# A linear-attention layer and a two-layer MLP on one core: the issue order from a list schedule, and the weights loaded as fp32 on the input queue

## The chip, the core and the metric

The kernel runs on one core of one Trainium2 chip. The metric is device time in microseconds of one execution; three runs of the kernel before gave a median of 226.93 us (226.46 to 227.11). Engines are named as in the profile: PE is TensorE (PEld its weight loads), DVE is VectorE, ACT is ScalarE, POOL is GpSimd, SP is SyncE, which here only issues transfers.

## What is computed

Inputs `r`, `k`, `v`, `w` of shape (4 batches, 8 heads, 768 steps, 48), `u` of (8, 48), and two weight matrices, all fp32.

```python
for t in range(S):
    cur = einsum('bhd,bhe->bhde', u[None] * k[t], v[t])
    y[t] = einsum('bhd,bhde->bhe', r[t], state + cur)
    state = w[t][:, :, :, None] * state + einsum('bhd,bhe->bhde', k[t], v[t])
x = y as 3072 tokens x 384
h = x @ moe_w_in                  # 384 x 2048
out = maximum(0.01 * h, h) @ moe_w_out   # 2048 x 384
```

## The kernel before

**Attention** is worked in chunks of 128 steps: 24 chunks (6 for each batch, in order, as the state is handed on). For a chunk ScalarE takes the log of `w` (`s_log`, L124), TensorE makes its running sums `cum` with two triangular matrices, ScalarE the exponentials, and VectorE the decayed `rd` and `kd` (`s_decay`, L129). TensorE transposes them (`trp`), VectorE copies them out (`rkT`), TensorE makes the scores `at`, VectorE masks them into `mt`, TensorE makes `y` from state and scores and the update `kv`, VectorE the sums `ysb` and `tt`, and GpSimd the new state `st` (`s_trans` to `s_mix`, L176 to L246). The `u` term goes beside it: three products on GpSimd (`t`, twice, and `vsc`), a cast of `v` (`vb`) and a sum on VectorE (`diag`) (L153 to L171). Last `ysb` is transposed (`ytr`) and ScalarE copies it into `xT` (`s_out`, L253).

**The MLP** works on blocks of tokens; ten blocks, `sizes = [384, 128, 128, 256, 384, 384, 384, 384, 384, 256]`. `m_hidden` (L269) makes `hp` from `w_in_b` and `xT`, three matmuls for each of 16 rows of tiles, and ScalarE writes the leaky ReLU to `gt`. `m_out` (L282) makes `op` for 128 tokens from 16 matmuls with `w_out_b`, ScalarE copies it (`osb`), and it is stored. `hp` and `op` share two PSUM buffers (`ps_mlp`).

**Loads.** SyncE's queue carries the four input tiles of each chunk (196.6 KB each, rows of 48 numbers) and the stores. Eight buffers for each input hold the chunks ahead. `load_w_in` (L105) and `load_w_out` (L113) read the fp32 weights on GpSimd's queue and turn them into bf16 on the way.

**Order.** Every engine works in the order of issue. That order is written by hand: each stage of each chunk has a position, the MLP's units are spread over the positions behind the chunks that they need, and all are sorted.

```python
def when(i, s):
    if i < 3:
        return 5 * i + s
    ...
    return 5 * i + 3 * s
...
events.append((when(2, 0) + 0.3, 0, 0, load_w_in, ()))
events.append((when(2, 0) + 0.4, 0, 0, load_w_out, ()))
```

The identity matrix `ident`, which the transposes need, is made on GpSimd at the program's start; its last step stands there behind the first product of chunk 0, which needs `u`.

Of the kernel before, what the change touches and what calls it, by code (L numbers as in the profile page):

```python
# [8 lines left out]
F32 = mybir.dt.float32  # L9
# [3 lines left out]
AX = mybir.AxisListType  # L13


@with_exitstack
def kernel(
# [47 lines left out]
    ident = const.tile([128, 128], BF16, name="ident")
    make_identity(nc, ident)
    ones = const.tile([128, 1], BF16, name="ones")
    nc.vector.memset(ones[:], 1.0)

# [5 lines left out]
    for t in lw_b + rd_b + kd_b:  # L75
        nc.vector.memset(t[:, :, D:64], 0.0)
    for t in st_b:
        nc.vector.memset(t[:], 0.0)

    nc.scalar.preload_act_table_set("natural_log_exp_and_others")  # L80

# [4 lines left out]


    ins = {}

    def load_chunk(i):  # L90
        b, c = divmod(i, C)
        t0 = c * L
        tiles = {}
        for name, src in (("w", w), ("r", r), ("k", k), ("v", v)):
            t = inpool.tile([128, H, D], F32, name=f"{name}_in", tag=f"{name}_in")
            nc.sync.dma_start(
                out=t[:], in_=src[b, :, t0 : t0 + L, :].rearrange("h p d -> p h d")
            )
            tiles[name] = t
        ins[i] = tiles  # L100
# [4 lines left out]
    def load_w_in():  # L105
        fq = FF // 4
        for q in range(4):
            nc.gpsimd.dma_start(
                out=w_in_b[:, :, q * fq : (q + 1) * fq],
                in_=moe_w_in[:, q * fq : (q + 1) * fq].rearrange("(t p) n -> p t n", p=128),  # L110
            )

    def load_w_out():  # L113
        hf = NFT // 2
        for q in range(2):
            nc.gpsimd.dma_start(
                out=w_out_b[:, q * hf : (q + 1) * hf, :],
                in_=moe_w_out[q * hf * 128 : (q + 1) * hf * 128, :].rearrange("(t p) n -> p t n", p=128),
            )


    att = {}

    def s_log(i):  # L124
        a = att[i] = ins.pop(i)
        a["lw"] = lw_b[i % NB3]
        nc.scalar.activation(out=a["lw"][:, :, 0:D], in_=a["w"][:], func=AF.Ln)  # L127

    def s_decay(i):  # L129
        c = i % C  # L130
        a = att[i]
        lw, rd, kd = a["lw"], rd_b[i % NB3], kd_b[i % NB3]
        a["rd"], a["kd"] = rd, kd
        cum = ps_cum.tile([128, 1024], F32, name="cum")
        nc.tensor.matmul(cum[:, 128:512], lhsT=tri[:], rhs=lw[:, :, 0:D], start=True, stop=True)  # L135
        nc.tensor.matmul(cum[:, 512:896], lhsT=trin[:], rhs=lw[:, :, 0:D], start=True, stop=True)  # L136
        for p in range(NP):
            nc.tensor.matmul(  # L138
                cum[:, 896 + p : 897 + p],
                lhsT=lw[:, 2 * p : 2 * p + 2, :].rearrange("p h d -> p (h d)"),  # L140
                rhs=ones[:], start=True, stop=True,
            )
        nc.scalar.activation(out=cum[:, 128:900], in_=cum[:, 128:900], func=AF.Exp)  # L143
        e1 = cum[:, 128:512].rearrange("p (h d) -> p h d", h=H)
        e2 = cum[:, 512:896].rearrange("p (h d) -> p h d", h=H)
        nc.vector.tensor_tensor(out=rd[:, :, 0:D], in0=e1, in1=a["r"][:], op=ALU.mult)  # L146
        nc.vector.tensor_tensor(out=kd[:, :, 0:D], in0=e2, in1=a["k"][:], op=ALU.mult)  # L147
        if c < C - 1:
            el = work.tile([128, NP], F32, name="el")
            nc.vector.tensor_copy(out=el[:], in_=cum[:, 896:900])  # L150
            a["el"] = el

    def s_prod(i):  # L153
        a = att[i]
        t1 = work.tile([128, DM], F32, name="t1", bufs=2)
        nc.gpsimd.tensor_tensor(out=t1[:], in0=a["r"][:].rearrange("p h d -> p (h d)"), in1=ukb[:], op=ALU.mult)  # L156
        t2 = work.tile([128, H, D], F32, name="t2", bufs=2)
        nc.gpsimd.tensor_tensor(  # L158
            out=t2[:], in0=t1[:].rearrange("p (h d) -> p h d", h=H), in1=a["k"][:], op=ALU.mult
        )  # L160
        a["t2"] = t2
        vb = work.tile([128, DM], BF16, name="vb")
        nc.gpsimd.tensor_copy(out=vb[:], in_=a["v"][:].rearrange("p h d -> p (h d)"))
        a["vb"] = vb

    def s_diag(i):
        a = att[i]
# [209 lines left out]
```

## Time and profile before

| what | value |
|---|---|
| median of 3 runs | 226.93 us |
| profiled execution | 227.73 us |
| its span, first to last instruction | 225.7 us |
| TensorE busy | 188.8 us (84%) |
| VectorE, ScalarE, GpSimd busy | 105.8, 109.6, 104.5 us |
| read and written in HBM | 25.36 MB, 4.72 MB |

All times within a profile count from the start of the span. How the rows of the next sections read: in a table of stretches, each row has the stretch, its length, then for PE, PEld, DVE, ACT and POOL the busy time with the number of instructions, then the granted TensorE clock (1.00 is full speed), the share of the DMA engines and GB/s. In a timeline a row has start, length, engine, line, operation, output<-input, shape, count, and in brackets the idle time before it with what ended it; rows of the queue of SyncE are marked SPq, and their length is that of the issue. A row of the chain has start, length, engine, name, line and count; its first line gives shares of the stretch. In rows by line, the last numbers are busy time and mean length in ns, then idle time before.

### The profile page before, as it was taken

The numbers are of one execution on the slowest core, as the hardware profiler recorded it, in microseconds if no ns is written. First come the engines' busy times: TensorE is split into PE (matmuls) and PEld (weight loads), VectorE is DVE, ScalarE is ACT, GpSimd is POOL, SyncE is SP. The second block draws the span as 40 slices with busy tenths as digits, with TensorE's granted clock in tenths as the row PEclk, the third lists the DMA queues.
The fourth block names the chain that finished last, engine by engine and source line by source line (L and its number), as shares of the span: only waits on it lengthen the run. The fifth ranks groups of instructions, "written<-read, shape, count | busy, mean of one in ns | idle before, by whom it ended". The sixth has DMA issues, their size and how long they took to land.

```text
span 225.7 us, 4666 instructions
## 1 busy us (share of the span) xinstructions
PE 188.8 (84%) x1816; PEld 124.0 (55%) x1816; DVE 105.8 (47%) x220; ACT 109.6 (49%) x217; POOL 104.5 (46%) x152
## 2 busy tenths in 40 slices
PE   1135454996995999899999999999999999999992
PEld 1123232554583867756666666666666666556761
DVE  2344361142450797767665476645756574420000
ACT  3111202682262655645863685478538833672540
POOL 2434597005183357776835457658175557110000
PEclk9999999999999699999999999999999999999998
DMA  7999999999898999888678566300021001100101
GB/s 132 198 189 186 188 180 181 187 184 198 160 196 214 227 164 195 180 147 182 135 134 170 139 119 100 107 35 3 0 73 37 3 23 47 38 0 35 73 0 71
DMA packets 107142, 27.24 MB, mean 121 GB/s; under 512 B 100336, under 2 KB 107120, under 8 KB 107120
## 3 DMA queue, kind: packets, MB, share of 16 engines
q1 hardware_dynamic: 103440, 23.80, 56.3%
q0 software_dynamic: 3680, 3.15, 8.7%
q8 instruction: 14, 0.23, 0.5%
q14 instruction: 8, 0.07, 0.1%
HBM read 25.36 MB, written 4.72 MB: 133 GB/s over the span
## 4 chain that ended last, share of the span: by engine, by line
PE 52%; ACT 2%; issue 0%; ACTq 0%
PE op L288 21%; PE hp L276 20%; PE trp L181 2%; PE at L195 2%; ACT gt L280 1%; PE y L221 1%; PE cum L135 1%; PE ytr L257 1%; PE cum L136 1%; PE y L215 1%; PE kv L234 1%; PE cum L138 0%; ACT osb L294 0%; ACT xT L258 0%; ACTq L294 0%
## 5 line engine op out<-in xcount | busy, mean ns | idle before, releaser
L276 PE MATMUL hp<-xT,w_in_b 128*128 128x384 bf16 (+2 forms) x480 | 78.2, 302 | 4.6 <-ACT osb L294 2.8
L280 ACT ACTIVATE gt<-hp 128x384 bf16<-128x384 f32 (+1 forms) x120 | 60.6, 512 | 22.2 <-PE hp L276 20.5
L288 PE MATMUL op<-w_out_b,gt 128*128 128x384 bf16 x384 | 69.0, 326 | 1.7 <-DMA w_out_b<-in_moe_w_out_dram 1.4
L276 PEld LDWEIGHTS <-w_in_b 128*128 128x128 bf16 x480 | 41.6, 100 | 24.3 <-issue 9.1
L288 PEld LDWEIGHTS <-gt 128*128 128x128 bf16 x384 | 35.5, 98 | 22.8 <-issue 2.2
L171 POOL TENSOR_TENSOR vsc<-v_in,diag 128x384 f32<-128x384 f32 x24 | 19.9, 829 | 47.0 <-DVE diag L169 47.0
L246 POOL TENSOR_TENSOR st<-tt,el 48x192 bf16<-48x192 f32 x40 | 20.1, 502 | 37.4 <-DVE tt L241 29.5
L201 DVE TENSOR_TENSOR mt<-at,tri 128x512 bf16<-128x512 f32 x48 | 30.7, 682 | 10.9 <-PE at L195 10.9
L146 DVE TENSOR_TENSOR rd<-cum,r_in 128x384 bf16<-128x384 f32 x24 | 13.4, 556 | 43.2 <-ACT cum L143 43.1
L294 ACT COPY osb<-op 128x384 f32<-128x384 f32 x24 | 11.5, 478 | 43.3 <-PE op L288 37.3
L156 POOL TENSOR_TENSOR t<-r_in,ukb 128x384 f32<-128x384 f32 x24 | 23.9, 997 | 7.8 <-DMA ukb<-in_u_dram 6.4
L258 ACT COPY xT<-ytr 128x384 bf16<-128x384 bf16 x24 | 11.4, 476 | 31.7 <-PE ytr L257 31.6
L227 DVE TENSOR_TENSOR ysb<-y,vsc 128x384 bf16<-128x384 f32 x24 | 13.4, 557 | 25.5 <-PE y L221 15.8
L143 ACT ACTIVATE cum<-cum 128x772 f32<-128x772 f32 x24 | 19.2, 799 | 12.6 <-issue 8.3
L158 POOL TENSOR_TENSOR t<-t,k_in 128x384 f32<-128x384 f32 x24 | 23.9, 996 | 1.8
L185 DVE COPY rkT<-trp 128x1024 bf16<-128x1024 bf16 x24 | 16.5, 689 | 16.7 <-PE trp L181 16.5
L181 PE MATMUL trp<-ident,rd 128*128 128x128 bf16 x96 | 10.1, 234 | 7.5 <-POOL ident masks.py:199 4.2
L135 PE MATMUL cum<-lw,tri 128*128 128x384 bf16 x24 | 8.4, 351 | 7.9 <-ACT lw L127 7.9
L195 PE MATMUL at<-rkT 48*128 48x128 bf16 x192 | 10.6, 229 | 3.7 <-DVE rkT L185 2.4
L127 ACT ACTIVATE lw<-w_in 128x384 bf16<-128x384 f32 x24 | 12.5, 521 | 1.8 <-DMA w_in<-in_w_dram 1.8
L147 DVE TENSOR_TENSOR kd<-cum,k_in 128x384 bf16<-128x384 f32 x24 | 13.1, 548 | 0.0
L169 DVE TENSOR_REDUCE diag<-t 128x8 f32<-128x384 f32 x24 | 13.0, 543 | 0.0
(39 smaller groups left out, 147.9 us busy)
## 6 DMA issues: line engine op xcount, KB each, us to landing
w_in<-in_w_dram SPq DMA_DIRECT2D x24, 192.0 KB, 4.5
r_in<-in_r_dram SPq DMA_DIRECT2D x24, 192.0 KB, 4.5
k_in<-in_k_dram SPq DMA_DIRECT2D x24, 192.0 KB, 4.5
v_in<-in_v_dram SPq DMA_DIRECT2D x24, 192.0 KB, 4.2
out_dram<-osb SPq DMA_DIRECT2D x24, 192.0 KB, 2.0
w_in_b<-in_moe_w_in_dram POOLq DMA_DIRECT2D x4, 384.0 KB, 9.0
w_out_b<-in_moe_w_out_dram POOLq DMA_DIRECT2D x2, 768.0 KB, 18.4
ukb<-in_u_dram SPq DMA_DIRECT2D x1, 192.0 KB, 4.5
```

What stands on the lines that cost most here:

```text
L143: nc.scalar.activation(out=cum[:, 128:900], in_=cum[:, 128:900], func=AF.Exp)
L156: nc.gpsimd.tensor_tensor(out=t1[:], in0=a["r"][:].rearrange("p h d -> p (h d)"), in1=ukb[:], op=ALU.mult)
L158: nc.gpsimd.tensor_tensor(out=t2[:], in0=t1[:].rearrange("p (h d) -> p h d", h=H), in1=a["k"][:], op=ALU.mult)
L171: nc.gpsimd.tensor_tensor(out=vsc[:], in0=a["v"][:], in1=diag[:].unsqueeze(2).to_broadcast([128, H, D]), op=ALU.mult)
L181: nc.tensor.transpose(trp[:, x, p, :], src[:, 2 * p : 2 * p + 2, :].rearrange("p h d -> p (h d)"), ident[:])
L185: nc.vector.tensor_copy(out=rkT[:], in_=trp[:])
L195: nc.tensor.matmul(ats[x][:, p, :], lhsT=rkT[r0 : r0 + D, 1, p, :], rhs=rkT[r0 : r0 + D, 0, p, :], start=True, stop=True,)
L201: nc.vector.tensor_tensor(out=mt[:, x], in0=ats[x][:], in1=tri[:].unsqueeze(1).to_broadcast([128, NP, 128]), op=ALU.mult)
L246: nc.gpsimd.tensor_tensor(out=sn[r0 : r0 + D, :, x * D : (x + 1) * D], in0=tt[r0 : r0 + D, :, x * D : (x + 1) * D], in1=a["el"][r0 : r0 + ...
L276: nc.tensor.matmul(hp[:, jj, :], lhsT=w_in_b[:, t, (j + jj) * 128 : (j + jj + 1) * 128], rhs=xT[:, t, t0 : t0 + mb], start=(t == 0), stop= ...
L280: nc.scalar.activation(out=gts[q][:, j : j + nj, :], in_=hp[:], func=AF.Prelu, alpha=0.01)
L288: nc.tensor.matmul(op[:], lhsT=gts[q][:, j, ts * 128 : (ts + 1) * 128], rhs=w_out_b[:, j, :], start=(j == 0), stop=(j == NFT - 1),)
```

## The change

1. The order of issue is now made by a list schedule (`Order`). Every step is added with its engine, a planned duration, the steps it needs and the PSUM buffers it takes. `run` then picks, over all engines, the step that could start first (ties by rank: attention by chunk, then the MLP), and so writes one order. The stages are cut into single steps, such as `rd`, `kd`, `rkT`, the two masks; `op` is cut into four parts instead of two.
2. The weights are loaded as fp32 on SyncE's queue, behind the inputs of chunk 3 and ahead of those of chunk 4, in eight loads of 786 KB, into four staging buffers. ScalarE casts `w_in` (three casts a load), VectorE `w_out` (one a load). A load of `w_out` reuses a staging buffer of `w_in`.
3. There are eight blocks, `[512, 128, 256, 384, 384, 384, 512, 512]`.
4. The constants, `ident` among them, are one step at the head of GpSimd's order. The output buffers are four instead of three.

The computation is otherwise the same.

```diff
+class Order:
+    def add(self, name, eng, took, f, *args, lag=0.06, rank=0.0, needs=(), takes=()):
+        self.steps[name] = (eng, took, f, args, lag, rank, list(needs), takes)
...
+        while any(todo.values()):
+            best = None
+            for eng, names in todo.items():
...
+                for rank, seq, name in names:
...
+                    t = ready(name)
+                    if t is None:
+                        continue
+                    t = max(t, free[eng])
+                    key = (t, rank, seq)
+                    if best is None or key < best[0]:
+                        best = (key, eng, (rank, seq, name))
...
+    wpool = ctx.enter_context(tc.tile_pool(name="wpool", bufs=4))
+    opool = ctx.enter_context(tc.tile_pool(name="opool", bufs=4))
...
-    def load_w_in():
-        fq = FF // 4
-        for q in range(4):
-            nc.gpsimd.dma_start(
-                out=w_in_b[:, :, q * fq : (q + 1) * fq],
-                in_=moe_w_in[:, q * fq : (q + 1) * fq].rearrange("(t p) n -> p t n", p=128),
-            )
...
+    def load_w_in(q):
+        t = wpool.tile([128, KT, FQ], F32, name="ws", tag="ws")
+        nc.sync.dma_start(
+            out=t[:], in_=moe_w_in[:, q * FQ : (q + 1) * FQ].rearrange("(t p) n -> p t n", p=128)
+        )
+        stage["in", q] = t
...
+    def cast_w_in(q, t):
+        nc.scalar.copy(out=w_in_b[:, t, q * FQ : (q + 1) * FQ], in_=stage["in", q][:, t, :])
+
+    def cast_w_out(q):
+        nc.vector.tensor_copy(out=w_out_b[:, q * JQ : (q + 1) * JQ, :], in_=stage["out", q][:])
...
-    sizes = [384, 128, 128, 256, 384, 384, 384, 384, 384, 256]
+    sizes = [512, 128, 256, 384, 384, 384, 512, 512]
...
+    add("const", "POOL", 2.2, constants, rank=-1)
+    queue = [("in", i) for i in range(4)]
+    queue[1:1] = [("u", 0)]
+    queue += [("w_in", q) for q in range(NQ)] + [("w_out", q) for q in range(NQ)]
+    queue += [("in", i) for i in range(4, NCH)]
...
+            add((kind, n), "DMA", 2.2, f, n, lag=1.9, needs=[("cast", "w_in", n)] if kind == "w_out" else [])
...
+        step("scores", "PE", 0.35, a_scores, "rkT", lag=0.1, takes=(("att", "m0"), ("att", "m1")))
+        step("m0", "DVE", 0.66, a_mask, "scores", *past(2, "mix"), args=(0,))
...
+            add(("hid", q, j), "PE", nj * 3 * (mb / 2400 + 0.003), m_hid, q, j, nj, lag=0.1, rank=100 + q,
+                takes=(("mlp", ("act", q, j)),),
...
+                add(("out", q, ts, part), "PE", JQ * 0.163, m_out, q, ts, part, lag=0.1, rank=101.5 + q + 0.01 * ts,
...
+    steps = order.run({"att": 3, "mlp": 2})
     with tc.manual_schedule():
...
+        for f, args in steps:
+            f(*args)
```

How the order moves, at three places. First the weights' loads. Before, they stand in GpSimd's order, behind the products and the cast of chunk 2 (`t_355` is its first product):

```order
L156 TENSOR_TENSOR t_355<-r_in,ukb 128x384
L158 TENSOR_TENSOR t_357<-t_355,k_in 128x384
L163 CAST vb<-v_in 128x384
L108 DMA w_in_b<-in_moe_w_in_dram 128x3x512 x4
L116 DMA w_out_b<-in_moe_w_out_dram 128x8x384 x2
L171 TENSOR_TENSOR vsc<-v_in,diag 128x384
```

With the change they stand on SyncE's queue; `v_in_336` is the last tile of chunk 3, `w_in_541` the first of chunk 4, and `ws` are the staging buffers:

```order
L177 DMA v_in_336<-in_v_dram 128x8x48
L189 DMA ws_363<-in_moe_w_in_dram 128x3x512
L189 DMA ws_393<-in_moe_w_in_dram 128x3x512
L189 DMA ws_422<-in_moe_w_in_dram 128x3x512
L189 DMA ws_441<-in_moe_w_in_dram 128x3x512
L196 DMA ws_474<-in_moe_w_out_dram 128x4x384
L196 DMA ws_485<-in_moe_w_out_dram 128x4x384
L196 DMA ws_504<-in_moe_w_out_dram 128x4x384
L196 DMA ws_523<-in_moe_w_out_dram 128x4x384
L177 DMA w_in_541<-in_w_dram 128x8x48
```

The weights have moved from GpSimd's queue to SyncE's, between chunks 3 and 4. Second, ScalarE around the end of chunk 3 with the change (`cum_340` is the exponential of chunk 3, `ytr_397` and `ytr_467` are the outputs of chunks 2 and 3, `ws_363` to `ws_441` the four loads of `w_in`):

```order
L230 ACTIVATE cum_340<-cum_340 128x772
L203 CAST w_in_b_101<-ws_363 128x512
L350 COPY xT_103<-ytr_397 128x3x128
L203 CAST w_in_b_101<-ws_363 128x512 x2
L203 CAST w_in_b_101<-ws_393 128x512 x3
L203 CAST w_in_b_101<-ws_422 128x512 x3
L350 COPY xT_103<-ytr_467 128x3x128
L203 CAST w_in_b_101<-ws_441 128x512 x2
L376 ACTIVATE gt_479<-hp_480 128x512
```

Nine of the new casts stand ahead of the copy that completes block 0, and two more ahead of the first `gt`. Third, ScalarE's end with the change, which mirrors TensorE's there (a `gt` follows each `hp` tile, an `osb` each tile of `op`):

```order
L350 COPY xT<-ytr 128x3x128
L376 ACTIVATE gt<-hp 128x512 x5
L350 COPY xT<-ytr 128x3x128
L376 ACTIVATE gt<-hp 128x512 x11
L389 COPY osb<-op 128x384 x3
L376 ACTIVATE gt<-hp 128x512 x16
L389 COPY osb<-op 128x384 x8
```

The last 27 tiles of `hp` (blocks 6 and 7) have no attention between them now, and their `op` tiles follow in two runs.

## Rows read from the trace of the kernel before

**Rows 1.** Table of stretches, all engines.

```profile
0.00:55.00 55.00, 28.24 (x210) 16.32 (x211) 19.44 (x49) 16.33 (x30) 24.86 (x41) 1.00 1.18 182
55.00:104.27 49.27, 43.86 (x530) 32.88 (x529) 30.16 (x61) 23.52 (x44) 27.99 (x40) 0.97 1.00 188
104.27:147.89 43.62, 43.58 (x430) 28.18 (x430) 25.93 (x52) 26.82 (x56) 25.24 (x35) 1.00 0.62 126
221.54:225.70 4.16, 0.00 (x0) 0.00 (x0) 0.00 (x0) 0.48 (x1) 0.00 (x0) 0.79 0.14 49
29.20:54.00 24.80, 17.66 (x119) 9.50 (x118) 8.35 (x18) 10.33 (x21) 12.51 (x17) 1.00 1.23 185
74.00:76.00 2.00, 1.83 (x18) 1.45 (x17) 1.93 (x5) 1.56 (x4) 0.00 (x0) 0.50 1.28 210
```

**Rows 2.** Timeline of ScalarE: the logs of chunks 1 and 2.

```profile
16.28 0.53 ACT L127 ACTIVATE lw<-w_in 128x384 bf16<-128x384 f32 x1
...
26.00 0.53 ACT L127 ACTIVATE lw<-w_in 128x384 bf16<-128x384 f32 x1
```

**Rows 3.** Timeline of SyncE's queue: issues of input tiles.

```profile
15.95 0.96 SPq L96 DMA_DIRECT2D v_in<-in_v_dram  x1
16.96 1.15 SPq L96 DMA_DIRECT2D w_in<-in_w_dram  x1
...
41.77 7.05 SPq L96 DMA_DIRECT2D w_in<-in_w_dram  x1
```

**Rows 4.** The weights' tiles: issues (first and last start), and `w_out` from issue to landing.

```profile
L108 POOL DMA_DIRECT2D w_in_b<-in_moe_w_in_dram x4: 772/775/927, 29.2 to 31.6; - x4
...
L116 POOL DMA_DIRECT2D w_out_b<-in_moe_w_out_dram x2: 881/897/913, 32.4 to 33.3; - x2
...
DMA to landing us min/median/max: 16.1/18.4/20.6
```

**Rows 5.** Timeline of the head: VectorE's first product, and four places on TensorE.

```profile
6.24 0.56 DVE L146 TENSOR_TENSOR rd<-cum,r_in 128x384 bf16<-128x384 f32 x1 [4.21 <-ACT cum L143]
...
9.55 0.58 PE L181 MATMUL trp<-ident,rd 128*128 128x128 bf16 x4 [4.18 <-POOL ident masks.py:199]
...
36.78 2.08 PE L276 MATMUL hp<-xT,w_in_b 128*128 128x384 bf16 x6 [0.57 <-ACT xT L258]
...
40.59 4.03 PE L276 MATMUL hp<-xT,w_in_b 128*128 128x384 bf16 x15
...
54.01 1.46 PE L288 MATMUL op<-w_out_b,gt 128*128 128x384 bf16 x8 [1.40 <-DMA w_out_b<-in_moe_w_out_dram]
```

**Rows 6.** Timeline of TensorE: a wait ahead of 104 us, and two block starts.

```profile
94.36 0.38 PE L195 MATMUL at<-rkT 48*128 48x128 bf16 x7 [0.78 <-DVE ysb L227]
...
104.27 0.65 PE L276 MATMUL hp<-xT,w_in_b 128*128 128x384 bf16 x3 [0.33 <-ACT xT L258]
...
147.89 0.65 PE L276 MATMUL hp<-xT,w_in_b 128*128 128x384 bf16 x3
```

**Rows 7.** The chain: shares of 104.27 to 147.89, and pieces of the end.

```profile
by line: PE hp L276 38.6%; PE op L288 36.5%; PE trp L181 5.9%; PE at L195 4.5%; PE y L221 2.7%; PE ytr L257 2.3%; PE cum L135 2.2%; PE cum L136 2.2%; PE kv L234 2.0%; PE y L215 1.9%; PE cum L138 1.1%; issue 0.2%
...
199.62 0.66 PE hp L276 x3
...
207.72 2.60 PE op L288 x16
210.32 5.93 PE hp L276 x48
```

**Rows 8.** The page's DMA queue of the weights, and issue to landing of `v`.

```profile
q0 software_dynamic: 3680, 3.15, 8.7%
...
v_in<-in_v_dram SPq DMA_DIRECT2D x24, 192.0 KB, 4.2
```

**Rows 9.** Groups by line and shape: a copy on ScalarE and one on VectorE.

```profile
L280 ACT ACTIVATE gt<-hp 128x512 bf16<-128x512 f32 x24 | 14.3, 597 | 7.8 <-PE hp L276 7.2
L185 DVE COPY rkT<-trp 128x1024 bf16<-128x1024 bf16 x24 | 16.5, 689 | 16.7 <-PE trp L181 16.5
```

More of the change, by code (lines that the diff above doesn't have):

```diff
@@ L113, in load_w_out @@
[L113 to L134, printed above, removed]
+    NQ = 4
@@ L147, in s_decay @@
[L147 to L157, printed above, removed]
+            nc.tensor.matmul(cum[:, 896 + p : 897 + p], lhsT=pair(lw, p), rhs=ones[:], start=True, stop=True)
@@ L192, in s_scores, with a_rkT, a_scores @@
+    def a_rkT(i):
+        rkT = att[i]["rkT"] = work.tile([128, 2, NP, 128], BF16, name="rkT")
+        nc.vector.tensor_copy(out=rkT[:], in_=att[i]["trp"][:])
+    def a_scores(i):
+        rkT = att[i]["rkT"]
+        ats = att[i]["ats"] = [ps_att.tile([128, NP, 128], F32, name=f"at{x}", tag="att") for x in range(2)]
         for p in range(NP):
@@ new lines, in a_kv, with a_tt @@
+    def a_kv(i):
+        kv = att[i]["kv"] = ps_att.tile([128, NP, 96], F32, name="kv", tag="att")
+        for p in range(NP):
+            nc.tensor.matmul(
+                kv[:, p, :], lhsT=pair(kd_b[i % NB3], p), rhs=att[i]["vb"][:, p * 96 : (p + 1) * 96],
+                start=True, stop=True,
+            )
+    def a_tt(i):
+        tt = att[i]["tt"] = work.tile([128, NP, 96], F32, name="tt", bufs=2)
+        if i % C > 0:
+            nc.vector.tensor_tensor(out=tt[:], in0=att[i]["kv"][:], in1=st_b[i % 2][:], op=ALU.add)
+        else:
+            nc.vector.tensor_copy(out=tt[:], in_=att[i]["kv"][:])
@@ new lines, in a_st, with a_ytr @@
+    def a_st(i):
+        sn, tt, el = st_b[(i + 1) % 2], att[i]["tt"], att[i]["el"]
+        for x in range(2):
+            r0 = 64 * x
+            nc.gpsimd.tensor_tensor(
+                out=sn[r0 : r0 + D, :, x * D : (x + 1) * D],
+                in0=tt[r0 : r0 + D, :, x * D : (x + 1) * D],
+                in1=el[r0 : r0 + D, :].unsqueeze(2).to_broadcast([D, NP, D]),
+                op=ALU.mult,
+            )
+    def a_ytr(i):
+        ytr = att[i]["ytr"] = ps_att.tile([128, KT, 128], BF16, name="ytr", tag="att")
+        for t in range(KT):
+            nc.tensor.transpose(ytr[:, t, :], att[i]["ysb"][:, t * 128 : (t + 1) * 128], ident[:])
@@ L264, with a_xT @@
+    def a_xT(i):
+        nc.scalar.copy(out=xT[:, :, i * L : (i + 1) * L], in_=att[i]["ytr"][:])
+        att[i].clear()
+        ins[i].clear()
+    sizes = [512, 128, 256, 384, 384, 384, 512, 512]
     assert sum(sizes) == B * S
@@ L339, with m_copy, m_store @@
-    events.sort(key=lambda e: e[:3])
-    with tc.manual_schedule():
-        load_chunk(0)
-        load_u()
-        for i in range(1, PRE):
-            load_chunk(i)
-        for _, _, _, f, args in events:
+    def m_copy(q, ts):
+        osb = osbs[q, ts] = opool.tile([128, NOUT], F32, name="osb")
+        nc.scalar.copy(out=osb[:], in_=ops.pop((q, ts))[:])
+    def m_store(q, ts):
+        row = starts[q] + ts * 128
+        nc.sync.dma_start(out=out[row : row + 128, :], in_=osbs.pop((q, ts))[:])
@@ new lines @@
+    order = Order()
+    add = order.add
+    add("const", "POOL", 2.2, constants, rank=-1)
[3 more added lines that the diff above has]
+    queue += [("in", i) for i in range(4, NCH)]
+    for kind, n in queue:
+        if kind == "in":
+            for x in ("w", "r", "k", "v"):
+                add((x, n), "DMA", 1.18, load_in, n, x, lag=1.9, needs=[("done", n - NIN)] if n >= NIN else [])
+        elif kind == "u":
+            add("u", "DMA", 0.5, load_u, lag=1.9)
+        else:
+            f = load_w_in if kind == "w_in" else load_w_out
+            add((kind, n), "DMA", 2.2, f, n, lag=1.9, needs=[("cast", "w_in", n)] if kind == "w_out" else [])
+            if kind == "w_in":
+                for t in range(KT):
+                    name = ("cast", kind, n) if t == KT - 1 else ("part", kind, n, t)
+                    add(name, "ACT", 0.48, cast_w_in, n, t, needs=[(kind, n)], rank=4.5)
+            else:
+                add(("cast", kind, n), "DVE", 1.7, cast_w_out, n, needs=[(kind, n)], rank=4.5)
```

374 lines of the change are left out of this document (213 added, 161 removed).

## The prediction

> **What bounds the kernel now.** I read the table of stretches first [rows 1]. From 104.27 to 147.89 us TensorE is busy 43.58 of 43.62 us. Before that it is not: in the first 55 us it is busy 28.2, so 26.8 are idle, and from 55 to 104.27 another 5.4. No other engine is near full in any stretch. So the questions are why TensorE starves early, and what its work costs where it doesn't.
>
> Three causes show in the head. (a) One chunk of attention at a time: the logs of chunks 1 and 2 on ScalarE begin at 16.28 and 26.00 us, each right behind the copy to `xT` of the chunk before [rows 2]. The inputs come faster: tiles are issued 1.0 us apart (15.95, 16.96) [rows 3], a chunk in some 4.1. (b) The weights are issued late, behind the GpSimd work of chunk 2: `w_in` from 29.2, `w_out` from 32.4 us, whose second half lands 20.6 us after its issue [rows 4]; an `op` group waits for it until 54.01 [rows 5]. (c) The first transposes begin at 9.55 after a wait of 4.18 us for `ident` [rows 5], though `rd` began at 6.24 and `kd`, right behind it, ended near 7.3.
>
> In the even part two blocks of 384 tokens, six chunks, begin at 104.27 and end where the next begins, at 147.89 [rows 6]: 43.6 us. The chain that ended last [rows 7] prices it: 16 `op` matmuls in a row take 2.60 us, 0.1625 each, and `hp` matmuls of 384 columns stream as many columns. The shares of the attention lines there add up to 24.8% of 43.62 us, 10.8, or 1.80 a chunk. Six chunks need 192 x 0.1625 + 10.8 = 42.0 us, so 1.6, or 0.27 a chunk, goes to small waits.
>
> **The change, part by part: when TensorE becomes dense.** The sum is: that moment, the TensorE work left then, its losses, the tail.
>
> Inputs of chunks 0 to 3 keep their place, so `v` of chunk 3, issued at 15.95 [rows 3], lands some 4.2 us later, the median of its kind [rows 8]: 20.2. `ident` now comes before any product, so the first transposes follow `kd` at 7.3. Chunks overlap now, and VectorE is the longest engine of a chunk: 25.93 us for six [rows 1], 4.3 each. Four of them from 6.24 end at 23.5; with the parts of a chain that can't overlap the last copy to `xT` could come at 25 to 28 us.
>
> Weights: eight loads of 786 KB follow at 20.2. What one costs in fp32 no row shows. While the old loads were in flight, 29.2 to 54.0, 185 GB/s moved [rows 1], 4.59 MB, of which 3.15 were weights [rows 8]; the other 1.44 MB are 7.3 tiles of 1.0 us, so the weights had some 17.2 us, 2.15 a load. Their share of the DMA engines, 8.7% of 225.7 us [rows 8], gives 19.6 us, 2.45 a load. The far end: if fp32 goes at the rate of the input tiles, 196.6 KB in 1.0 us [rows 3], a load takes 4.1. I take 2.3, since these loads have long packets like the old ones (3.15 MB in 3,680, some 860 bytes each [rows 8]; an input packet is a row of 48 fp32 numbers). The Trainium skill, "DMA: Bandwidth & Descriptors", section "Anatomy of one DMA", gives a fixed part and 436 GB/s, an estimate of 1.80 a load; by it the third load of `w_in` would land 1.5 us earlier and the sum would fall by as much at most. No run here shows it.
>
> At 2.3 the loads of `w_in` land at 22.5, 24.8, 27.1 and 29.4. ScalarE casts each in three; a cast of 512 columns isn't in the trace, its neighbour is 0.597 us for 512 columns from PSUM [rows 9]: 0.6. The casts of the first three loads stand ahead of the copy of chunk 3, which ends at 27.1 + 1.8 + 0.5 = 29.4: **dense from 29.5 us** (28.5 with faster loads, 31 with slower). Two casts of the fourth load stand ahead of the first `gt`; they end at 30.6, when the first `hp` is only just done.
>
> A load of `w_out` waits for the cast that frees its staging buffer, with all later inputs queued behind it on SyncE. The first such cast ends near 25, the fourth near 32, while the loads ahead keep the DMA engines at work until 29.4 and 36.3: no hole, with some 4 us of cover. Should ScalarE be later than that, each us goes to chunk 4 and all after it. `w_out` lands until 38.6. VectorE casts it in four pieces of 1,536 columns (1.0 us each at the rate of `rkT` [rows 9], twice that if it runs at half of it) between chunks 3 and 4, when it has nothing else.
>
> Chunk 4 arrives 17 us later than before, near 43. TensorE has the 64 + 48 long matmuls of block 0 (512 tokens) until past 50, so most of that chunk's attention, some 9 us long, is covered.
>
> **What is left at 29.5.** `op`: 384 x 0.1625 = 62.4. `hp`: the same number of columns in fewer matmuls, 62.4. Attention of 20 chunks: 36.0. Together 160.8 us. Losses:
> - The first dense matmuls run at half speed: six of 384 columns took 2.08 us at 36.78 and 15 took 4.03 at 40.59 [rows 5], 2.7 us over 21 x 0.1625. (The granted clock there reads 1.00; only after an idle piece, in 74 to 76, does it read 0.50, the 1.2 GHz level [rows 1]. I go by the durations.) I take 2.0, as a part hides in the next loss.
> - `hp` with nothing between its tiles waits for ScalarE: 48 matmuls of 256 columns took 5.93 us [rows 7], 0.741 for a tile of 512 against 4 x 0.1625 = 0.650. The order now has some 43 such tiles (blocks 0, 6 and 7): 3.9. By the tile of 384, 0.66 where 0.49 would do [rows 7], it would be 9.
> - Small waits: 0.27 a chunk x 20 = 5.4; between 0 and 0.5, some way up to the single wait of 0.78 in the crowded stretch ahead of 104 us [rows 6], that is 10.
>
> Tail, from the last matmul: 221.54 to 225.70, 4.2 us [rows 1], unchanged, as the last piece is a tile of 128 tokens in both.
>
> Sum: 29.5 + 160.8 + 2.0 + 3.9 + 5.4 + 4.2 = 205.8 us of span. The profiled execution had a span of 225.7 in 227.73, so 207.8, and the median of the runs was 0.8 under it: **207.0 us**. The bounds of the terms reach from 198 (28.5; losses 1, 2 and 0) to 219 (31; 2.7, 9 and 10).
>
> **Rivals.**
> 1. **The weights hold the inputs up.** A tile's issue that took 1.0 us took 7.05 during the old loads [rows 3], so the two shared the same engines; here the chunks simply queue behind. If a load takes 4.1 us, `w_out` is there at 53, chunk 4 at 57, and TensorE, with block 0's first twelve `op` matmuls done at 45, waits for the transposes of chunk 4 until about 60: 15 us lost, 222. Each 0.1 us above 2.5 a load costs 0.8 of arrival, of which the first 2 us are covered. Against it: what the old loads cost. 0.12, from 211 to 222. "DMA: Bandwidth & Descriptors" of the Trainium skill, section "Issuing engines are not separate DMA queues", has it as a rule that all issuers end on the same 16 engines; by that rule, the trace agrees, the move to SyncE's queue buys no bandwidth, only an earlier start.
> 2. **The order ties TensorE to the chains (slower).** Every step of every engine is placed by planned costs, and an engine that waits holds all that stands behind it. The new order puts 20 chunks between 42 us and the last 49 us of pure `hp` and `op`, some 5.4 us each, where the even part gave them 7.27; against VectorE's 4.3 the masks and scores of a chunk have little slack. From 1.0 us of extra wait in each of 20 chunks, (227.7 - 207.8) / 20, the gain is gone; at 1.3 it gives 233. That the crowded stretch of before shows waits like the 0.78 [rows 6] speaks for some of it; against it, that its steps stood by a formula of their number and not by what they wait for. 0.07.
> 3. **No change.** It would need what the head saves to be lost in the middle, with VectorE as the pace from 42 us on: 20 chunks x 4.3 end at 128, at 5 us a chunk at 142, and the 49 us behind them end before 195. So it takes 1 and a part of 2 together: 0.03.
>
> **How the numbers follow.** The forecast has 0.78; its own range is 200 to 214. To leave out no more than 2 in 10 I take in the better part of rival 1: 200 to 217. A measurement of this kernel can tell about 0.3% from no change. Faster by more than that: the forecast and nearly all of rival 1, 0.89; within it 0.03; slower 0.08.
>
> **What would show it.** In the new profile: the last weights landed near 39; the first `hp` at 29 to 30 and no idle piece of TensorE over 1 us behind it, above all none between 42 and 60; the 16 `hp` tiles of block 7 in about 11.9 us; the last matmul at 200 to 203. It is wrong by rival 1 if weight loads land more than 3 us apart and the transposes of chunk 4 wait; by rival 2 if TensorE's waits for VectorE and ScalarE behind the head add up to 20 us; by a mis-sized term if the first `hp` is late by more than 2 us.

## The result and the profile after

The changed kernel takes **207.37 us** (median of 4 runs, 207.12 to 208.92) beside 227.02 us for the kernel before in the same session: a ratio of 0.915, 95% interval [0.910, 0.920]. The profiled execution took 207.23 us with a span of 205.4. The forecast was 207.0.

TensorE's busy time hardly moved, 188.8 to 187.5 us, while its idle time fell from 36.9 to 17.9 us (span less busy): 19.0 of the 20.3 us that the span lost. The table of stretches after the change shows where. The columns are those of [rows 1].

```profile
0.00:55.00 55.00, 41.35 (x334) 23.88 (x335) 30.84 (x68) 29.55 (x51) 27.48 (x46) 1.00 0.96 229
55.00:104.00 49.00, 48.92 (x588) 34.76 (x587) 39.19 (x81) 33.95 (x69) 37.32 (x53) 1.00 1.03 177
44.00:201.83 157.83, 157.18 (x1507) 99.04 (x1504) 85.77 (x172) 90.21 (x175) 78.82 (x111) 1.00 0.66 124
```

In the first 55 us TensorE is idle for 13.7 us, where it was 26.8; from 55 to 104 us for 0.1, where it was 5.4 [rows 1]; from 44.00 to its last matmul at 201.83 for 0.65 in all. VectorE's row shows what moved: 39.2 us of work from 55 to 104, where it had 30.2, as the attention of all chunks is now drawn forward and done near 153. Its total rose only from 105.8 to 108.8 us, the four casts included.

ScalarE's timeline shows both halves of the head, the overlapped chunks and the casts:

```profile
9.25 0.52 ACT L218 ACTIVATE lw<-w_in 128x384 bf16<-128x384 f32 x1 [3.03 <-DMA w_in<-in_w_dram]
...
14.53 0.53 ACT L218 ACTIVATE lw<-w_in 128x384 bf16<-128x384 f32 x1
...
23.88 0.62 ACT L203 CAST w_in_b<-ws 128x512 bf16<-128x512 f32 x1 [2.75 <-DMA ws<-in_moe_w_in_dram]
24.40 0.47 ACT L350 COPY xT<-ytr 128x384 bf16<-128x384 bf16 x1
24.77 2.92 ACT L203 CAST w_in_b<-ws 128x512 bf16<-128x512 f32 x5
28.04 1.66 ACT L203 CAST w_in_b<-ws 128x512 bf16<-128x512 f32 x3 [0.35 <-DMA ws<-in_moe_w_in_dram]
29.61 0.47 ACT L350 COPY xT<-ytr 128x384 bf16<-128x384 bf16 x1
```

The logs of chunks 1 and 2 start at 9.25 and 14.53, where they started at 16.28 and 26.00 [rows 2]; the first now waits only for its input. Nine casts then stand ahead of the last copy to `xT`, at 29.61. SyncE's queue and TensorE's timeline behind it:

```profile
16.87 3.83 SPq L189 DMA_DIRECT2D ws<-in_moe_w_in_dram  x4
25.94 8.44 SPq L196 DMA_DIRECT2D ws<-in_moe_w_out_dram  x4
34.43 0.50 SPq L177 DMA_DIRECT2D w_in<-in_w_dram  x1
```

```profile
6.87 0.61 PE L271 MATMUL trp<-ident,rd 128*128 128x128 bf16 x4 [1.48 <-DVE rd L234]
...
28.97 0.50 PE L347 MATMUL ytr<-ident,ysb 128*128 128x128 bf16 x3 [0.40 <-DVE ysb L316]
30.13 12.82 PE L370 MATMUL hp<-xT,w_in_b 128*128 128x512 bf16 x45 [0.65 <-ACT xT L350]
...
43.86 2.11 PE L382 MATMUL op<-w_out_b,gt 128*128 128x384 bf16 x12
45.81 0.39 PE L271 MATMUL trp<-ident,rd 128*128 128x128 bf16 x4
```

The loads of `w_out` were held back by their staging buffers: their four issues last from 25.94 to 34.4, with chunk 4's first tile right behind. TensorE's first transposes no longer wait for `ident`, its first `hp` starts at 30.13 (before 36.78, [rows 5]), and neither the first `op` nor the transposes of chunk 4 have a wait in brackets. The chain that ended last, start and end of the dense part:

```profile
30.13 4.51 PE hp L370 x12
34.67 1.46 PE hp L370 x6
...
161.27 7.80 PE op L382 x48
169.07 11.87 PE hp L370 x48
180.94 20.89 PE op L382 x128
```

Four tiles in a slow start (1.13 us each), then 0.73 a tile; at the end 16 tiles of block 7 in 11.87 us; the last matmul ends at 201.83, 3.6 us before the span does.

### The profile page after: what moved, and what is told of

The parts are those of the page before. It is cut to its first block, busy times and chain, and to the rows that moved or that the text cites. A ratio compares the mean times of both kernels' runs of the same rounds, so it can differ in the third digit from the quotient of the medians.

```text
span 205.4 us, 4462 instructions
## 1 busy us (share of the span) xinstructions
PE 187.5 (91%) x1720; PEld 115.4 (56%) x1720; DVE 108.8 (53%) x224; ACT 115.1 (56%) x217; POOL 99.1 (48%) x146
## 4 chain that ended last, share of the span: by engine, by line
PE 81%; SPq 8%; DMA 5%; ACT 2%; issue 1%; DVE 1%; ACTq 0%
PE hp L370 33%; PE op L382 31%; SPq L177 7%; DMA ws<-in_moe_w_in_dram 5%; PE trp L271 4%; PE at L283 3%; PE y L308 2%; PE ytr L347 2%; PE cum L223 2%; PE cum L224 2%; PE kv L321 1%; PE y L302 1%; ACT w_in_b L203 1%; SPq L189 1%; ACT gt L376 1%
## 5 line engine op out<-in xcount | busy, mean ns | idle before, releaser
L370 PE MATMUL hp<-xT,w_in_b 128*128 128x384 bf16 (+3 forms) x384 | 76.2, 331 | 1.4 <-ACT xT L350 0.7
L376 ACT ACTIVATE gt<-hp 128x512 bf16<-128x512 f32 (+1 forms) x108 | 58.8, 550 | 19.5 <-PE hp L370 17.1
L382 PE MATMUL op<-w_out_b,gt 128*128 128x384 bf16 x384 | 68.0, 326 | 0.0
L370 PEld LDWEIGHTS <-w_in_b 128*128 128x128 bf16 x384 | 33.5, 98 | 30.2 <-issue 11.5
L234 DVE TENSOR_TENSOR rd<-cum,r_in 128x384 bf16<-128x384 f32 x24 | 13.3, 553 | 11.1 <-ACT cum L230 10.9
L254 POOL CAST vb<-v_in 128x384 bf16<-128x384 f32 x24 | 12.1, 503 | 5.0 <-DMA v_in<-in_v_dram 4.8
```

Of the source, the lines that this page charges most:

```text
L370: nc.tensor.matmul(hp[:, jj, :], lhsT=w_in_b[:, t, (j + jj) * 128 : (j + jj + 1) * 128], rhs=xT[:, t, t0 : t0 + mb], start=(t == 0), stop= ...
L376: nc.scalar.activation(out=gts[q][:, j : j + nj, :], in_=hps.pop((q, j))[:], func=AF.Prelu, alpha=0.01)
L382: nc.tensor.matmul(ops[q, ts][:], lhsT=gts[q][:, j, ts * 128 : (ts + 1) * 128], rhs=w_out_b[:, j, :], start=(j == 0), stop=(j == NFT - 1),)
```

## The experiments

The theory at the start was the prediction's: the gain is the earlier start of the dense part, paid out one to one, less the small losses that it prices. It came to be wrong in one respect: an earlier first `hp` is not paid out one to one, and can bring nothing or a loss. Experiments 2, 3, 7 and 9 show it. The changed kernel measured 207.37 us and the kernel before 226.9 to 227.2 in all sessions; each ratio is to the kernel before.

### 1. The form and the queue of the loads

The changed kernel with its weights read as bf16 on GpSimd's queue, at the same place of the order, without staging or casts.

```diff
-        t = wpool.tile([128, KT, FQ], F32, name="ws", tag="ws")
-        nc.sync.dma_start(out=t[:], in_=moe_w_in...)
+        nc.gpsimd.dma_start(out=w_in_b[:, :, q * FQ : (q + 1) * FQ], in_=moe_w_in...)
```

> The changed kernel with the weights as bf16 by GpSimd's queue, eight loads at the same planned place (behind chunk 3's inputs), no staging buffers and no casts. Theory A (queue and type of the load do not matter, only when it starts): 206 to 209 us; the casts ahead of xT of chunk 3 are gone, but the loads share the DMA engines with chunks 4 and 5. Rival D (a queue of its own lets the loads and the inputs of chunks 4 to 6 slow each other, as tiles that took 4.75 and 7.05 us to issue did before): w_in lands 3 us later or more, 210 to 214 us.

Measured: 207.95 us, 0.915 [0.914, 0.917]; the first `hp` at 29.84. **So half of the change's title, fp32, SyncE's queue and the casts, is worth nothing by itself.** Rival D's condition came about, but not its time: GpSimd issued the loads of `w_in` between its products, from 21.2 to 27.1, where SyncE had issued them from 16.9 to 19.1. They landed 5.9 to 8.6 us after their issues (7.0 to 10.9 in the changed kernel), so 3 to 6 us later than there. TensorE, which takes `w_in` a quarter at a time, still didn't wait for them. ScalarE's last copy to `xT` ahead of the first `hp` waits for the chunk alone here:

```profile
29.31 0.48 ACT L345 COPY xT<-ytr 128x384 bf16<-128x384 bf16 x1 [5.02 <-PE ytr L342]
```

### 2. Early weights in the old order

The kernel before, with the fp32 loads on SyncE behind chunk 3, eight staging buffers and the casts.

```diff
+            if i == 3:
+                load_w_in()
+                load_w_out()
...
-    events.append((when(2, 0) + 0.3, 0, 0, load_w_in, ()))
-    events.append((when(2, 0) + 0.4, 0, 0, load_w_out, ()))
+    events.append((when(2, 4) - 0.1, 0, 0, cast_w_in, ()))
+    events.append((when(3, 0) - 0.05, 0, 0, cast_w_out, ()))
```

> The kernel before with one part of the change: weights as fp32 on SyncE's queue behind chunk 3 (eight staging buffers, so no load waits), cast by ScalarE and VectorE; its order otherwise as it was. Theory A (TensorE has to become dense early, which needs the first block's xT and the weights; the serial chunks hold xT): the first hp still begins near 36.8 us, since xT of chunk 2 ends at 36.7 there; only the waits for w_out (about 3 us between 50 and 54) and some of the late inputs go: 221 to 225 us. Rival B (the earlier weights by themselves make the gain): 207 to 213 us.

Measured: 227.37 us, 1.002 [0.999, 1.004]. Neither theory held: no gain at all. The first `hp` came 1.1 us earlier (35.67 for 36.78 [rows 5]), and no `op` waited for `w_out` any more. What took the gain is further on. TensorE's and ScalarE's timelines of this run, and SyncE's queue ahead of them:

```profile
73.89 1.44 PE L291 MATMUL hp<-xT,w_in_b 128*128 128x128 bf16 x12 [5.20 <-ACT osb L309]
```

```profile
73.36 0.48 ACT L309 COPY osb<-op 128x384 f32<-128x384 f32 x1 [6.45 <-DMA out_dram<-osb]
```

```profile
68.66 1.05 SPq L98 DMA_DIRECT2D v_in<-in_v_dram  x1
69.84 2.03 SPq L311 DMA_DIRECT2D out_dram<-osb  x3
```

The fourth copy of an output waits 6.45 us for one of the three `osb` buffers, whose stores stand on SyncE's queue behind input tiles and go out only at 69.84. ScalarE is held with all that is queued behind it, and then TensorE for 5.20 us. In the kernel before the same copy waited 4.09 us, and TensorE 2.83. In this run, what came there sooner waited longer.

### 3. Overlapped chunks in the old order

```diff
-        if i < 3:
-            return 5 * i + s
+        if i < 4:
+            return 2.5 * i + s
```

> The kernel before with one line of its hand-written order changed: chunks 0 to 3 get positions 2.5 i + s instead of 5 i + s (and the old rule for chunk 3), so that their stages interleave; weights on GpSimd's queue as before, which that rule also issues earlier, behind the products of chunk 2. No list schedule, no casts. Theory A (the overlap of the chunks in the head is what pays): xT of chunk 2 ends near 25 us, w_in lands near 30, the first hp begins near 30 to 32 and TensorE is dense from there; the fixed positions behind it keep the waits of the crowded stretch (5 us): 209 to 215 us. Rival E (the list schedule of the whole program is needed, because the middle gives the gain back): over 218 us.

Measured: 226.09 us, 0.994 [0.992, 0.997]; my theory missed by 11 us or more, and the time is in rival E's range. TensorE's timeline and one stretch of this run:

```profile
28.60 0.48 PE L215 MATMUL y<-st,rkT 128*128 128x96 bf16 x4 [5.44 <-POOL st L246]
...
69.99 0.48 PE L135 MATMUL cum<-lw,tri 128*128 128x384 bf16 x1 [4.71 <-ACT lw L127]
```

```profile
60.00:80.00 20.00, 14.85 (x186) 11.12 (x185) 11.88 (x24) 7.23 (x13) 9.92 (x14) 0.83 1.15 206
```

The first `hp` came at 33.93, only 2.9 us earlier, since the weights' loads stand on GpSimd ahead of `st`, which TensorE then waits for 5.44 us. And the middle takes the rest: from 60 to 80 us TensorE is idle 5.15 us, with the granted clock at 0.83. ScalarE's copy of an output waits 5.66 us for a store here too, and holds the log that `cum` waits for.

### 4. The new order with the chunks of the head in series

```diff
-        step("log", "ACT", 0.52, a_log, "w", *past(3, "cum"))
+        step("log", "ACT", 0.52, a_log, "w", *past(3, "cum"), *(past(1, "xT") if i < 4 else []))
```

> The changed kernel, but the log of chunks 1 to 3 waits for the copy to xT of the chunk before, as the old order had it. Theory A (chunks that overlap in the head make most of the gain): a chunk takes 9.7 us as before, xT of chunk 3 ends near 14.6 + 3 x 9.7 = 43.7 us instead of 30, the first hp follows, and part of it is taken back as chunk 4 is worked beside: 217 to 221 us. Rival B (earlier weights make the gain): under 210 us.

Measured: 221.25 us, 0.974 [0.971, 0.976], 0.25 us past the theory's end. The first `hp` moves from 30.13 to 45.86, 15.7 us, and the time by 13.9.

### 5. The new order with late weights

The loads behind chunk 6 instead of 3; so that no bank is held for long, an `op` part 0 also waits for its block's last `hp`.

```diff
-    queue = [("in", i) for i in range(4)]
+    queue = [("in", i) for i in range(7)]
...
-                    + ([("out", q, ts, part - 1)] if part else []))
+                    + ([("out", q, ts, part - 1)] if part else [("hid", q, NFT - nj)]))
```

> The changed kernel with the weights behind chunk 6 instead of chunk 3 on SyncE's queue (28 tiles ahead of them instead of 16), and the first op part of a block made to follow the block's last hp. Theory A: the loads of w_in land at 32.5 to 39.5 us, the first hp begins near 34 to 35 and is paced by the loads; in the meantime TensorE does the attention of chunks 4 to 6 (1.8 us each), so little is lost: 208 to 212 us. Rival B (where the weights stand makes the gain): the 12 us by which they come later are lost, 216 to 220 us.

Measured: 215.52 us, 0.948 [0.947, 0.950]; 8.2 us lost (with the `op` edit), between the two theories' ranges. The first `hp` is 10.9 us later (41.01), and the attention of three more chunks in that time gives some 3 x 1.8 = 5.4 back. The other 2.7 or so aren't settled. A part may be the casts, which now stand among the `gt` of block 0, as in this piece of ScalarE's timeline; from the first `hp` to the first `op` the run takes 17.9 us (to 58.90), for 13.7, though with some matmuls of block 1 between:

```profile
47.42 0.61 ACT L203 CAST w_in_b<-ws 128x512 bf16<-128x512 f32 x1
47.93 1.11 ACT L376 ACTIVATE gt<-hp 128x512 bf16<-128x512 f32 x2
48.93 0.61 ACT L203 CAST w_in_b<-ws 128x512 bf16<-128x512 f32 x1
49.44 1.23 ACT L376 ACTIVATE gt<-hp 128x512 bf16<-128x512 f32 x2
```

### 6. Wrong planned durations

All of the change is kept; only the durations that the planner is told for VectorE's nine kinds of step are halved.

```diff
-        step("m0", "DVE", 0.66, a_mask, "scores", *past(2, "mix"), args=(0,))
+        step("m0", "DVE", 0.330, a_mask, "scores", *past(2, "mix"), args=(0,))
```

> The changed kernel planned with half of the true durations for all VectorE steps of attention; the work is the same, only the order differs. Rival 2 of the prediction (the order ties TensorE to the chains, so a plan that is wrong costs): the planned chunks follow each other faster than VectorE can work, TensorE's attention steps stand too early and wait: 0.3 to 1 us more for each of 20 chunks, 213 to 228 us. If the order absorbs it (queues run ahead, any order near this one does): under 210 us.

Measured: 228.02 us, 1.005 [1.002, 1.007]. **The whole gain is gone, with the same instructions.** Stretches of this run:

```profile
60.00:80.00 20.00, 17.06 (x218) 12.39 (x217) 13.29 (x26) 9.90 (x19) 11.85 (x17) 1.00 0.83 156
...
104.00:150.00 46.00, 42.35 (x462) 26.32 (x460) 35.59 (x72) 29.14 (x59) 31.23 (x44) 1.00 0.91 156
150.00:200.00 50.00, 48.42 (x356) 25.16 (x354) 16.28 (x31) 28.05 (x53) 14.55 (x21) 1.00 0.27 56
```

TensorE stands idle 2.9 us in 60 to 80 and 3.7 in 104 to 150, in many small waits for `mt`, `rkT` and `rd`, and VectorE still has 16.28 us of attention to do behind 150, where the changed kernel has under a microsecond (below). The first `hp` is 3.2 us late too (33.28). The idle time is not the whole loss: TensorE also shows as busy for 196.2 us with the same instructions, where it had 187.5 (experiment 12 shows how a wait can hide there). This is rival 2's mechanism; the right durations keep it away here.

### 7. The old block sizes

The ten old sizes in the new order (with the `op` edit of experiment 5).

```diff
-    sizes = [512, 128, 256, 384, 384, 384, 512, 512]
+    sizes = [384, 128, 128, 256, 384, 384, 384, 384, 384, 256]
```

> The changed kernel with the ten old blocks (384, 128, 128, 256, 5 x 384, 256), and the first op part of a block made to follow the block's last hp. If what stands ahead of the first hp sets the end (theory A): block 0 needs only chunks 0 to 2, so its first hp can begin near 25 us when the first load of w_in is cast; 3 to 4 us earlier, paced by the loads until 31, with the attention of chunk 3 (1.8 us) still to do, and only 8 tiles of hp alone at the end (19 fewer, 0.09 us each): 203 to 206 us. Rival F (small blocks starve TensorE behind block 0, as chunk 4 comes at 43 us): 208 to 212 us.

Measured: 210.67 us, 0.927 [0.925, 0.930]: rival F's time, and the theory missed. Yet the first `hp` came at 26.25, 3.9 us earlier, as the theory had it, and rival F's starving isn't seen: from 43.21, the first `op`, to 60 TensorE is idle for 0.5 us. Its idle time is small and spread: 1.4 us in 60 to 80, 1.4 in 150 to 200, waits for `gt` (1.1 us), `ysb`, `xT` and a cast. A part of the loss is at the end, where not 8 but 36 tiles of `hp` stand alone, 28 of them of only 384 columns. The 16 tiles of one block:

```profile
169.56 10.01 PE L370 MATMUL hp<-xT,w_in_b 128*128 128x384 bf16 x48
179.41 7.96 PE L382 MATMUL op<-w_out_b,gt 128*128 128x384 bf16 x48
```

They take 9.85 us to the start of `op`, where 48 x 0.1625 = 7.80 would do. In the chain from 44.00 to 201.83 `gt` has 7.5% here and 1.0% in the changed kernel.

### 8. A late `ident`

```diff
+    add("ident", "POOL", 0.5, make_identity, nc, ident, rank=0, needs=[("t1", 0)])
...
-        step("trans", "PE", 0.45, a_trans, "rd", "kd", *past(1, "rkT"), lag=0.1)
+        step("trans", "PE", 0.45, a_trans, "rd", "kd", ("ident",), *past(1, "rkT"), lag=0.1)
```

> The changed kernel with ident made behind the first product of chunk 0 on GpSimd, as in the kernel before; nothing else. In the changed kernel the copy to xT of chunk 3 and the casts ahead of it end together, at 29.6 us. Theory G (the attention chain binds there): the first transposes begin 2.3 to 2.5 us later, so does each chunk behind, and the end comes 1.5 to 2.5 us later: 209 to 210 us. Rival H (the loads and casts bind, the chain has slack): within 0.5 us of the changed kernel, 207 to 208 us.

Measured: 210.35 us, 0.925 [0.924, 0.926], 3.0 us lost. The first transposes start at 9.74 instead of 6.87, behind a wait of 4.39 us, and the first `hp` at 32.26 instead of 30.13. So the chain of attention has no slack there, as theory G says; in the changed kernel it and the casts end within 0.3 us of each other. The third microsecond was lost between the first `op` (45.84, 2.0 late) and the `op` of block 6 (164.25 for 161.27), where the planner wrote another order; by which wait wasn't found.

### 9. Weights still earlier

`w_in` ahead of chunks 2 and 3, `w_out` ahead of chunk 4, a first block of 256 tokens; the casts of `w_in` also get a rank of 1.5 for 4.5.

```diff
+    queue = [("in", 0), ("u", 0), ("in", 1)]
+    queue += [("w_in", q) for q in range(NQ)] + [("in", 2), ("in", 3)]
...
+    sizes = [256, 256, 128, 256, 384, 384, 384, 512, 512]
```

> The changed kernel, with the loads of w_in ahead of chunks 2 and 3 and those of w_out ahead of chunk 4, and a first block of 256 columns, not 512, so that the MLP could start behind chunk 1 and not chunk 3. Theory (dense work starts when xT of the first block and the first quarter of w_in are there, and the order then keeps TensorE fed): first hp at 25 to 27 us instead of 30.13, and 203 to 206 us. Rival K (what is gained ahead is lost behind: chunks 2 to 4 come about 8 us later, and the products run out of finished chunks before 60 us): 206.5 to 212 us, with waits of over 1 us on xT or rd between 30 and 60 us.

Measured: 210.34 us, 0.928 [0.924, 0.931]; rival K's time, though no single wait reaches its 1 us. The first `hp` starts at 19.47, even earlier than expected, and it is given back and more:

```profile
29.50:44.00 14.50, 11.11 (x102) 6.14 (x100) 11.60 (x20) 3.54 (x7) 6.30 (x7) 0.76 1.04 288
```

In the stretch where the changed kernel runs block 0 from 30.13 on without a break, TensorE has 3.4 us of holes, and the granted clock is 0.76 as a mean of the stretch. An early start alone is not the aim: **what counts is how early TensorE is fed and stays so.**

### 10. Warm-up products

Ten steps on TensorE, each of two products that nobody reads, ahead of the first `hp`.

```diff
+    for x in range(10):
+        add(("warm", x), "PE", 0.64, m_warm, x, lag=0.1, rank=50, takes=(("mlp", ("warm", x)),),
+            needs=[("kv", 2), ("cum", 3)] + ([("warm", x - 1)] if x else []))
```

> The changed kernel, with twenty products of 384 columns whose results nobody reads, in pairs, in TensorE's holes between chunk 2's kv and the first hp; the outputs are the same. Theory of the prediction (the first four hp tiles run at half speed because TensorE had stood still about half of the time ahead of them, a loss of 2.0 us, or 2.2 by the trace): the four tiles take 2.7 us and not 4.5, and the time is 205.2 to 206.2 us. Rival L (the products of chunk 3's attention queue behind them on TensorE, which is in order, and at half speed a pair takes 0.64 us: the first hp comes 1 to 2 us later): 206.8 to 209 us.

Measured: 207.55 us, 0.915 [0.912, 0.917]; no gain, rival L's time. Yet the cause of the slow start is confirmed by the chain of this run:

```profile
32.34 1.46 PE hp L375 x6
33.83 1.45 PE hp L375 x6
```

The first four tiles take 3.03 us (from 30.80, the first `hp`, to 33.83, where the fifth begins), where they took 4.54 (30.13 to 34.67). From the first `hp` to the first `op` the run needs 12.36 us (30.80 to 43.16) instead of 13.73; but the first `hp` is 0.67 late, so 0.7 is left, and 0.43 of it is there at the start of block 7 (168.64 for 169.07), which is less than the runs' spread.

### 11. More banks where `hp` runs alone

The first 13 tiles of block 0, block 6 from its sixth tile on and block 7 use attention's three PSUM banks.

```diff
+    def in_att(q, j):
+        return (q == 0 and j < 13) or (q == 6 and j > 4) or q == 7
...
+        if in_att(q, j):
+            hp = hps[q, j] = ps_att.tile([128, nj, mb], F32, name="hp", tag="att")
```

> The changed kernel, with the hp tiles of block 0 (the first 13 of 16), of block 6 (from its sixth on) and of block 7 in attention's three PSUM banks, which stand empty there, and no longer in the two banks for hp, so that up to three products can stand ahead of ScalarE's gt. Theory of the prediction (where hp runs alone, each tile waits about 0.09 us for ScalarE to give a bank back, which is my term of 3.9 us for 43 tiles): two thirds to all of that goes, 203.5 to 205.5 us. Rival J (the rate of hp alone is that of ScalarE's own gt, 0.60 us and a gap of its own, so more banks only let TensorE run ahead by one tile): 206.5 to 207.6 us.

Measured: 206.42 us, 0.909 [0.907, 0.911]; between the theories. The chain's end shows that the waits do go:

```profile
154.55 7.80 PE hp L376 x36
162.35 7.80 PE op L388 x48
170.15 10.36 PE hp L376 x48
```

48 matmuls take 10.36 us instead of 11.87, 36 take 7.80, and 0.65 a tile is the rate of the stream itself. But the planner, told of the free banks in block 0, wrote another order for the middle, in which TensorE is idle 1.6 us from 60 to 104 (42.40 busy of 44.00, where the changed kernel has 43.92), and block 7 starts 1.1 us later than in the changed kernel. Block 0 won little: its first `op` starts at 43.56 for 43.86, and in the changed kernel 0.4 us of chunk 4's `cum` stands ahead of it. Its tiles no longer wait, but the slow start lasted longer: the first four `gt` start 1.28 us apart, from 31.64 to 35.48.

### 12. The same, with the changed kernel's order untouched

Without block 0; the order on every engine is then the changed kernel's own.

```diff
+        return (q == 6 and j > 4) or q == 7
```

> The changed kernel, in its own order on every engine, with one thing changed: the hp tiles of block 6 from its sixth on and of block 7 stand in attention's three PSUM banks, which no chunk uses any more there (block 0 keeps its two banks, unlike the run before). Theory of the prediction, by the run before (block 7's 16 tiles then took 10.36 us instead of 11.87, 12 of block 6's 7.80 instead of 8.96, and what was lost on the way came from a different order between 60 and 104 us): 1.5 and 1.1 us go, 204.5 to 205.1 us, below both kernels. Rival M (the first product of a bank that attention gives up late waits there, or the op behind block 7 waits for the gt that ScalarE now makes later): 205.8 to 207.4 us.

Measured: **204.45 us**, 0.901 [0.897, 0.904], below both kernels, with its interval clear of the changed kernel's [0.910, 0.920]. The chain's end, and the last stretch of the changed kernel and then of this one:

```profile
160.38 7.80 PE op L388 x48
168.44 10.09 PE hp L376 x46
178.54 20.82 PE op L388 x128
```

```profile
150.00:200.00 50.00, 49.75 (x273) 25.54 (x272) 0.90 (x2) 24.00 (x43) 0.00 (x0) 1.00 0.11 40
```

```profile
150.00:200.00 50.00, 49.23 (x283) 26.70 (x283) 1.22 (x3) 24.65 (x44) 0.00 (x0) 1.00 0.12 44
```

One of block 7's 48 `hp` matmuls has no record in this trace; by the timeline they take 10.36 us, from the first at 168.01 to the `op` behind them at 178.37. The last run of `op` starts at 178.54 instead of 180.94. TensorE shows as busy in both stretches: **a wait of 0.09 us between two tiles isn't seen as idle time in such a table; it is seen in the length of the run.**

## Why the prediction was right, step by step

**Dense from 29.5.** It was 30.13, but two terms met there and the sum had one. The loads came at 349 and 347 GB/s in the two slices of the page between 20.5 and 30.8 us, so 786 KB took 2.26 us where the sum had 2.3. The Trainium skill's estimate, from "DMA: Bandwidth & Descriptors", section "Anatomy of one DMA", which describes the path of GpSimd's queue, was 1.80; the measurement decides against it here. The casts took 0.615 us on ScalarE (0.6 taken) and 0.96 on VectorE (1.0 to 2.0). The last three casts ahead of `xT` wait 0.35 us for the third load and start at 28.04, where the sum had 27.1. But the chain of the chunks, which the sum had ready at 25 to 28, was as late: `ytr` of chunk 3 ends at 29.47 in the changed kernel. In experiment 1, which has no casts, the last copy starts at 29.31 and the first `hp` at 29.84. So faster loads would have brought some 0.3 us at most, and that the time of the loads alone gave nearly the right moment is in part luck.

**The cover of 4 us.** It was thinner than said, and it was not what mattered. The last load of `w_out` was held until the fourth load of `w_in` was cast, 34.0 us (the sum said near 32), so the last weights landed at 40.5, for 39. TensorE had the `hp` of block 0 until 43.86, and chunk 4 wasn't waited for. Rival 1 did not come about. The rule in the Trainium skill's "DMA: Bandwidth & Descriptors", section "Issuing engines are not separate DMA queues", by which another queue buys no bandwidth, agrees with experiment 1: 29.84 and 30.13 for the first `hp`, 207.95 and 207.37 us.

**160.8 us of work and 11.3 of losses.** Together 172.1; from 30.13 to 201.83 it was 171.7. The term "small waits 5.4, or 0.27 a chunk" can be checked behind 44.00, where nearly all work of the 20 chunks stands: 157.83 us, less `op` 62.4, seven blocks of `hp` 52.0, attention 36.0 and 27 lone tiles x 0.09 = 2.4, leave 5.0. Only 0.65 of that is idle time of TensorE. The chain of this stretch, read as [rows 7] was for the 1.80, shows how the time divides (the view cuts the line off):

```profile
by line: PE op L382 40.0%; PE hp L370 34.1%; PE trp L271 5.7%; PE at L283 4.2%; PE y L308 2.7%; PE ytr L347 2.2%; PE cum L223 2.1%; PE cum L224 2.0%; PE kv L321 1.8%; PE y L302 1.6%; ACT gt L376 1.0%; PE cum L226 0.9%; DVE mt L291 0.9%; iss
```

The rows of attention add up to 23.2%, 36.6 us or 1.83 a chunk, so that price held. `op` has 63.1 us and `hp` 53.8, and 2.7%, 4.3 us, run through other engines or `issue`, `gt` (the lone tiles' among it) and `mt` ahead. So the 5.0 has the size and, by this chain, for the most part the kind that the term foresaw, though TensorE shows as busy for most of it. The kernel before is alike: `hp` and `op` have 38.6% and 36.5% of 43.62 us in [rows 7], 16.8 and 15.9, where 96 x 0.1625 = 15.6 would do for each. So its 1.6 us of small waits lies inside a stretch in which TensorE is busy 43.58 of 43.62 us [rows 1]: a busy column doesn't rule waits out. How much each single wait costs wasn't tested.

**`hp` alone waits for ScalarE, 43 tiles x 0.09.** Confirmed in place and size for the last 27 (for block 0's tiles experiment 11 shows only that the waits go): (11.87 - 16 x 0.65) / 16 = 0.09, and experiment 12 took 2.4 us out up to the last run of `op` (180.94 to 178.54), the 27 x 0.09 of the term, and 2.9 between the medians. That two banks are the cause, and not ScalarE's rate (0.597 a `gt`), is shown by experiments 11 and 12.

**The slow start, 2.0.** It was 4.51 - 4 x 0.65 = 1.9. Experiment 10 shows the cause, TensorE's idle time ahead of it, and that no more than 0.7 of it could be had that way.

**The tail, 4.2.** It was 3.6; the cause of the 0.6 wasn't looked for.

Two figures of the working are slightly off, and the sum goes by neither (its upper bound uses the 9): 24.8 less 7.3 us leaves 17.5 for the old loads, 2.19 a load and not 2.15; and by the tile of 384 the loss of 43 lone tiles is 7.4 us if it goes by the tile (43 x 0.17), 9.9 if it goes by the column, not 9.

**Where my understanding was short.** The prediction treats the order as a risk (rival 2) and the early start as the gain. The experiments that undo one part each lose 0.6 (fp32 and queue, within the spread), 8.2 (place of the weights, with an edit to `op`), 13.9 (overlap), 20.7 (true durations), 3.3 (sizes, with an edit to `op`) and 3.0 us (`ident`), far more than 19.6 together; and early weights or overlap alone, in the old order, bring 0 and 1 us. So the parts are not terms of a sum. For early weights and overlap both sides were measured: they are worth their price only while the rest holds. For the others only the loss was, and each such edit can also make the planner write another order. That the old order gave its gains back at one place, the store behind input tiles near 70 us, is shown as a wait in experiments 2 and 3; that a fourth `osb` buffer or an earlier store would free the old order is argued only, it wasn't tried. Nor was the old order with both head changes at once.

## What to carry to other kernels

Before an earlier start is counted as a gain, follow it to the next fixed point of the order, here a store queued behind loads, and ask if what comes sooner only waits longer there. A planned order is worth no more than its durations: with one engine's halved, all of the 20 us was gone; and an edit that only frees a resource can lose its gain when the planner writes a new order, so hold the order fixed when you measure it. When a matmul stream runs alone against another engine's drain, divide its length by its count: waits of 0.09 us are in no idle column, and a third bank took them away.

## What was not expected of the hardware

In the head the granted clock reads 1.00 while the first matmuls take far longer than later ones: 12 in 4.51 us, then 6 in 1.46; before, six of 384 columns in 2.08 [rows 5] where 0.98 would do. Only the durations show it.
